# Attention weights in the memory of k, b, w and a of a recurrence, loaded and split in its last tile

## Chip, cores, metric

One core of a Trainium2 chip. The metric is the device time of one execution in microseconds (us), median over runs.

## What is computed

The reference chains three parts: a recurrence over 768 time steps with a 40x40 state for each of 4 x 8 heads, a feed-forward part with a 3-tap convolution in time and a sigmoid gate, and a causal attention with 4 experts of which the best 2 are mixed for each token.

```python
for t in range(S):                      # B=4, H=8, S=768, D=40
    y[:, :, t] = einsum('bhd,bhde->bhe', rt, state)
    Sa = einsum('bhde,bhe->bhd', state, at)
    state = state * wt[:, :, None, :] - einsum('bhd,bhe->bhde', Sa, bt) + einsum('bhd,bhe->bhde', vt, kt)
...
h = maximum(x @ w_in, 0); c = conv3(h, conv_w); x = (h * sigmoid(c)) @ w_out      # 320 -> 1024 -> 320
...
logits = x @ w_gate; topk = the 2 largest of 4; w = softmax over them
for e in range(4):                      # q, k, v of 64 columns
    a = softmax(causal(scale * (x @ wq[e]) @ (x @ wk[e]).T))
    out += (weight of e if it is in topk) * (a @ (x @ wv[e]) @ wo[e])
```

## The kernel before, in words

The recurrence is cut into NT = 12 tiles of 64 steps. For each tile n, `prep(n)` (L167) turns the loaded k, b, w and a into chunk matrices, `chain(k)` (L331) carries the state over each of its two halves (k = 2n, 2n+1), and `post(k)` (L414) forms the outputs, which go to a DRAM scratch `xs` (L462). `w` and `kb` are single tiles and `a` a pair that alternates; `F` and `g21` are scratch of `prep`. `P` is a ring of three tiles: tile n uses P[n % 3].

The feed-forward part `ff` (L517) follows a tile behind. It goes in 49 steps: of each tile of 64 tokens, four steps multiply by `w_in` (L561), filter (L594, L596), gate (L598, L599), split the result into a high and a low half (`split`, L477: ACT copies the high half, another engine subtracts it, L478 and L479) and multiply by `w_out` (L584); `halves` (L534) splits the tile's input into xh and xl at each first step. `store` (L619) writes to a DRAM scratch `x2`.

The attention has `setup_c` (L629), which allocates its pools in the memory that the recurrence gives back, and `proj` (L672), which loads tokens from `x2` as xt (L678), transposes them (L694), splits them into x, and multiplies by the weights wvg (v and gate, L703) and wqk (q and k, L712). The keys' tile `k` holds high halves and `kl` low halves, with the other expert's 64 partitions zero. `weigh` (L748), `scale`, `turn`, `values` and `result` (weights wo, L830) go over units (batch b, block i of 128 queries, pair pr of experts).

In `setup_c`, after four small constants (cidb and negm on the POOL queue, L640 and L641; cid and bef on the SP queue, L642 and L643), eight rows of weights are loaded from DRAM into three staging tiles `ws` (L647, queue SP) and split by ACT (L478) and VectorE (L479): 3 of wvg with 260 columns, 3 of wqk with 512, 2 of wo with 320. Then POOL clears the unused halves of the two `kl` tiles with four memsets (L653).

The order of work comes about in two steps. The program's order is made by generators: each `yield` gives a position in units of tiles, and `Kernel.merge` (L895) always takes the stream with the lowest position; the feed-forward part is put in by the amount of matmul work done so far. The remaining `ff` steps and `proj` are merged in `attention` (L914). Then the compiler's planner (`schedule_with_timeline_sim`, L1018) puts the instructions on each engine's queue by priority and a simulated time of its own. At run time each queue is in order: PE, DVE (VectorE), ACT (ScalarE), POOL (GpSimd), and SP, whose queue starts nearly all DMAs. Tiles are protected by semaphores; a tile in memory that a closed pool has given back waits for the work on that pool.

## Time and profile before

| | |
|---|---|
| median of 3 runs | 898.44 us (894.2 to 899.88) |
| the profiled execution | 899.17 us |
| its span, first to last instruction | 897.4 us |
| busy share of the span | PE 83%, PEld 73%, DVE 77%, ACT 64%, POOL 42% |
| chain that ended last, by engine | PE 42%, DVE 24%, ACT 11%, DMA 10%, issue 7%, POOL 4% |
| mean granted clock of TensorE | 0.923 of full speed |

Times in rows are us from the span's start unless they are marked ns. A wait is booked on the engine that stood idle, with what ended it behind the arrow. Matmul durations overlap, since matmuls are pipelined, so sums of busy PE time are an upper bound of its work.

### The profile page before, as it was taken

What the parts mean: (1) busy time and instruction counts of PE and PEld (TensorE: products, weight loads), DVE (VectorE), ACT (ScalarE), POOL (GpSimd) and SP (SyncE); (2) the same over time, 40 slices, a digit from 0 to 9 for tenths busy, and PEclk for the clock granted to TensorE, in tenths of its full rate; (3) what the DMA queues carried; (4) which work ended last, traced back from release to release, by engine and by line L of the source; (5) the groups of instructions that cost most, each with busy time, mean ns of one, the idle gap of its engine ahead of it and who ended that gap; (6) DMA issues with size and microseconds to landing.
All of it is one profiled execution on the core that took longest, in us unless ns stands there. A gap on an engine that the chain in (4) does not pass through costs nothing.

```text
span 897.4 us, 31509 instructions
## 1 busy us (share of the span) xinstructions
PE 748.3 (83%) x13112; PEld 657.7 (73%) x13112; DVE 693.9 (77%) x1541; ACT 574.4 (64%) x1355; POOL 377.6 (42%) x419
## 2 busy tenths in 40 slices
PE   1257768997988989888798879869999999999988
PEld 1146556785877977777687868859878888888876
DVE  5888896999898898787887984575677767876664
ACT  0156655866675767584758567758877666775565
POOL 6063545433335243322334242754644343443352
PEclk9999577997989799897979889979999999999999
DMA  5435673555564464545545534440011101110001
GB/s 129 94 122 125 166 167 86 134 127 127 116 158 104 99 152 108 132 99 130 129 113 120 117 86 93 90 127 16 15 46 37 46 16 31 37 38 16 23 8 38
DMA packets 143489, 81.17 MB, mean 90 GB/s; under 512 B 113859, under 2 KB 127043, under 8 KB 142387
## 3 DMA queue, kind: packets, MB, share of 16 engines
q1 hardware_dynamic: 138450, 74.34, 34.1%
q0 software_dynamic: 4896, 4.83, 2.5%
q8 instruction: 103, 1.69, 0.8%
q14 instruction: 40, 0.32, 0.1%
HBM read 51.63 MB, written 11.80 MB: 71 GB/s over the span
## 4 chain that ended last, share of the span: by engine, by line
PE 42%; DVE 24%; ACT 11%; DMA 10%; issue 7%; POOL 4%; SPq 1%; ACTq 0%; DVEq 0%; POOLq 0%
PE ps L161 8%; PE ps L561 5%; PE ps L584 5%; PE ps L815 4%; DVE cv L596 4%; PE ps L712 4%; PE ps L798 4%; PE ps L165 3%; PE ps L703 2%; PE ps L762 2%; PE ps L830 2%; DMA kb<-in_kb_e_dram 2%; DVE kb L205 2%; PE ps L763 2%; DVE Q L198 2%
## 5 line engine op out<-in xcount | busy, mean ns | idle before, releaser
L784 POOL TENSOR_TENSOR A<-A,rs 128x128 f32<-128x128 f32 (+5 forms) x96 | 87.7, 935 | 113.7 <-DVE rs L782 95.6
L596 DVE SCALAR_TENSOR_TENSOR cv<-h,cw,cv 128x256 f32<-128x256 f32 (+1 forms) x192 | 97.1, 550 | 38.5 <-ACT cv L594 37.7
L599 POOL TENSOR_TENSOR cv<-cv,h 128x512 f32<-128x512 f32 (+1 forms) x48 | 61.4, 1280 | 133.2 <-ACT cv L598 123.6
L561 PE MATMUL ps<-xl,win 128*128 128x256 f32 x384 | 97.1, 304 | 4.5 <-POOL xl L539 3.6
L561 PE MATMUL ps<-xh,win 128*128 128x256 f32 x384 | 96.5, 309 | 4.9 <-ACT xh L537 4.3
L584 PE MATMUL ps<-wout,gh 128*128 128x320 f32 x384 | 90.4, 330 | 2.6 <-ACT gh L478 2.5
L479 POOL TENSOR_TENSOR gl<-cv,gh 128x512 fp32r<-128x512 f32 x48 | 62.5, 1303 | 53.5 <-ACT gh L478 46.9
L769 ACT ACTIVATE A<-ps,nm 128x128 f32<-128x128 f32 (+5 forms) x96 | 60.7, 633 | 37.0 <-DVE nm L767 28.9
L561 PEld LDWEIGHTS ps<-xh,win 128*128 128x128 f32 x384 | 73.2, 210 | 7.0 <-ACT xh L537 4.6
L561 PEld LDWEIGHTS ps<-xl,win 128*128 128x128 f32 x384 | 73.1, 208 | 6.0 <-POOL xl L539 4.1
L767 DVE TENSOR_REDUCE nm<-ps 128x1 f32<-128x128 f32 (+5 forms) x96 | 58.8, 619 | 20.5 <-PE ps L765 8.9
L584 PEld LDWEIGHTS ps<-wout,gh 128*128 128x128 f32 x384 | 66.0, 200 | 4.9 <-ACT gh L478 4.1
L161 PE MATMUL ps<-kb,a 40*32 40x64 f32 x1536 | 34.3, 239 | 34.7 <-DVE kb L205 31.1
L584 PE MATMUL ps<-wout,gl 128*128 128x320 f32 x192 | 59.0, 330 | 0.3 <-issue 0.3
L165 PE MATMUL ps<-cst,kb 104*128 104x104 f32 x192 | 33.3, 307 | 29.4 <-ACT KB L265 16.4
L161 PE MATMUL ps<-RB,LB 104*40 104x32 f32 (+1 forms) x1536 | 47.9, 215 | 11.1 <-DMA RB<-in_rb_dram 5.0
L161 PEld LDWEIGHTS ps<-kb,a 40*32 40x32 f32 x1536 | 28.1, 120 | 39.0 <-issue 19.1
L161 PEld LDWEIGHTS ps<-RB,LB 104*40 104x40 f32 (+1 forms) x1536 | 41.6, 131 | 17.3 <-DVE cv L596 4.6
L798 PE MATMUL ps<-cid,A 128*128 128x128 f32 x336 | 52.9, 276 | 1.5 <-ACT AT L803 0.7
L762 PE MATMUL ps<-k,q 128*128 128x256 f32 (+3 forms) x144 | 49.3, 351 | 5.3 <-ACT A L769 3.8
L712 PE MATMUL ps<-x,wqk 128*128 128x384 f32 x256 | 53.2, 347 | 0.3 <-ACT yt L622 0.3
L598 ACT ACTIVATE cv<-cv 128x512 f32<-128x512 f32 (+1 forms) x48 | 30.3, 630 | 30.7 <-DVE cv L596 30.4
(177 smaller groups left out, 2191.6 us busy)
## 6 DMA issues: line engine op xcount, KB each, us to landing
kb<-in_kb_e_dram SPq DMA_DIRECT2D x24, 320.0 KB
LB<-KB SPq DMA_DIRECT2D x48, 160.0 KB
LB<-S SPq DMA_DIRECT2D x46, 100.0 KB
a<-in_a_e_dram SPq DMA_DIRECT2D x24, 160.0 KB
VT<-in_vt_dram SPq DMA_DIRECT2D x48, 80.0 KB
RB<-in_rb_dram SPq DMA_DIRECT2D x48, 80.0 KB
SV<-in_v_dram SPq DMA_DIRECT2D x48, 80.0 KB
VZ<-in_v_dram SPq DMA_DIRECT2D x96, 40.0 KB
```

What stands on the lines that cost most here:

```text
L161: self.nc.tensor.matmul(*a, **k)
L165: self.nc.tensor.transpose(*a)
L479: (eng or self.nc.vector).tensor_tensor(lo, x, hi.bitcast(F32), op=ALU.subtract)
L561: nc.tensor.matmul(hp[:, dd], wt[:, 128 * d:128 * d + 128], x, start=k == 0, stop=k == 7)
L584: nc.tensor.matmul(self.ps[1][:, tb, :DM], x, wt, start=d == 0 and k == 0, stop=d == 7 and k == 2)
L596: nc.vector.scalar_tensor_tensor(y, h[:, dd, :, k:k + nt], self.cw[:, k, d:d + 1], y, op0=ALU.mult, op1=ALU.add)
L599: (nc.gpsimd if GM and st % GM == 0 and st >= GN else nc.vector).tensor_tensor(cv[:, :, :, :nt], cv[:, :, :, :nt], h[:, :, :, 1:1 + nt], o ...
L712: nc.tensor.matmul(pp, self.wqk[:, wk, hl, 128 * m:128 * m + 128], x[:, xk], start=j == 0, stop=j == 7)
L762: nc.tensor.matmul(sp[:, c0:c1], q[:, ce, 128 * j:128 * j + 128], k[:, ce, c0:c1], start=True, stop=False)
L769: nc.scalar.activation(A[:, :nk], sp[:, :nk], AF.Exp, bias=nm, accum_out=sums[:, e:e + 1])
L784: nc.gpsimd.tensor_tensor(A[:, :nk], A[:, :nk], rs[:, e:e + 1].to_broadcast([128, nk]), op=ALU.mult)
L798: nc.tensor.transpose(tp[:, m, e], As[e][:, 128 * (2 * g + m):128 * (2 * g + m) + 128], self.cid)
```

## The change

Two tiles s0 and s1 are made in a pool `shr` of their own, which lives to the end. In the recurrence s0 holds kb and w, s1 holds a[0], F and g21 (the pair's other tile a[1] stays). A new stream `more` calls `weights_c` from position 11.0 on, in steps of 0.15 tiles up to 12.05. It takes the two tiles again as wqk (s0) and wvg and wo (s1), and stages the eight rows in the two halves of P[0] (last used by tile 9). The split's subtraction is given to POOL in place of VectorE, and wqk comes first. `setup_c` keeps the four constants and the tiles kl, without loads and memsets. The memsets of kl for batch 0 go to VectorE in `proj(0, 0)`; those for batch 1 stay on POOL, in `weigh(1, 0, 0)`, queued behind the last subtraction of `halves` (`self.cut`). `bef` is allocated earlier.

```diff
-        self.w = cp.tile([128, 32, 32], F32, name="w")
-        self.kb = cp.tile([128, 16, 2, 2, 32], F32, name="kb")
-        self.a = [cp.tile([128, 2, 2, 16, 32], F32, name=f"a{j}") for j in range(2)]
+        s0, s1 = [self.sp.tile([128, n], F32, tag=f"s{j}", name=f"s{j}", bufs=1) for j, n in enumerate((3072, 2840))]
+        self.kb = s0[:, :2048].rearrange(...)
+        self.w = s0[:, 2048:].rearrange(...)
+        self.F = s1[:, 2048:2560].rearrange(...)
+        self.g21 = s1[:, 2560:2816].rearrange(...)
+        self.a = [s1[:, :2048].rearrange(...), cp.tile([128, 2, 2, 16, 32], F32, name="a1")]
...
-        F = wk.tile([128, 16, 32], F32, name="F", bufs=1)
+        F = self.F
...
-            nc.gpsimd.tensor_tensor(xl[64:, 2], xd[64:, 2], xh[64:, 2].bitcast(F32), op=ALU.subtract)
+            self.cut = nc.gpsimd.tensor_tensor(xl[64:, 2], xd[64:, 2], xh[64:, 2].bitcast(F32), op=ALU.subtract)
...
+    def weights_c(self):
+        s0, s1 = [self.sp.tile([128, n], F32R, tag=f"s{j}", name=f"r{j}", bufs=1) for j, n in enumerate((3072, 2840))]
+        self.wqk = s0.rearrange("p (k h n) -> p k h n", k=3, h=2)
+        self.wvg = s1[:, :1560].rearrange("p (k h n) -> p k h n", k=3, h=2)
+        self.wo = s1[:, 1560:].rearrange("p (k h n) -> p k h n", k=2, h=2)
+        P = self.P[(NT - 3) % 3].rearrange("p u t -> p (u t)")
+        j = 0
+        for dst, nm, n, rows in ((self.wqk, "w_qk", 512, 3), (self.wvg, "w_vg", 260, 3), (self.wo, "w_o", DM, 2)):
+            for k in range(rows):
+                s = P[:, 512 * (j % 2):512 * (j % 2) + n]
+                j += 1
+                nc.sync.dma_start(s, self.i[nm][k])
+                self.split(dst[:, k, 0], dst[:, k, 1], s, nc.gpsimd)
+                yield
...
-        for dst, nm, n, rows in ((self.wvg, "w_vg", 260, 3), (self.wqk, "w_qk", 512, 3), (self.wo, "w_o", DM, 2)):
-            for k in range(rows):
-                s = cw.tile([128, S], F32, tag="A", name="ws", bufs=3)[:, :n]
-                nc.sync.dma_start(s, i[nm][k])
-                self.split(dst[:, k, 0], dst[:, k, 1], s)
...
-        for t in self.kl:
-            for e in range(2):
-                nc.gpsimd.memset(t[Z[1 - e], e::2].bitcast(F32), 0.0)
...
             t["kl"] = self.kl[b % 2]
+            if b == 0:
+                for e in range(2):
+                    nc.vector.memset(t["kl"][Z[1 - e], e::2].bitcast(F32), 0.0)
...
+        if (b, i, pr) == (1, 0, 0):
+            with self.tc.issue_after(self.cut.ins):
+                for e in range(2):
+                    nc.gpsimd.memset(t["kl"][Z[1 - e], e::2].bitcast(F32), 0.0)
...
+            self.sp = top.enter_context(tc.tile_pool(name="shr", bufs=1))
             self.setup_b(bctx)
...
+                def more():
+                    yield NT - 1.0
+                    for j, _ in enumerate(self.weights_c()):
+                        yield NT - 1.0 + 0.15 * (j + 1)
+
-                self.merge([links(), preps(), second(), posts(), weights()], ff)
+                self.merge([links(), preps(), second(), posts(), weights(), more()], ff)
```

## Rows read from the trace of the kernel before

**Rows 1.** Stretches: length, busy us (count) of PE, PEld, DVE, ACT, POOL; clock; DMA.

```profile
541.00:576.00 35.00, 34.31 (x776) 31.38 (x764) 19.62 (x37) 26.52 (x60) 15.18 (x15) 1.00 0.42 92
576.00:607.00 31.00, 21.23 (x128) 19.15 (x128) 20.33 (x37) 18.11 (x46) 20.54 (x20) 0.83 0.47 120
607.00:630.00 23.00, 22.36 (x159) 21.63 (x159) 11.60 (x32) 18.80 (x41) 10.95 (x13) 1.00 0.06 15
```

**Rows 2.** PE's waits from 576 to 610: total us, times, longest.

```profile
PE ps L694 <- DMA x<-yt: 5.4, 1, 5.4
PE ps L703 <- DVE lg L706: 2.5, 1, 2.5
PE ps L584 <- ACT gh L478: 0.8, 1, 0.8
```

**Rows 3.** View of stretches of 5 us, columns as in rows 1.

```profile
585.00:590.00 5.00, 2.78 (x10) 2.06 (x11) 4.32 (x5) 1.19 (x4) 2.93 (x3) 0.51 0.63 182
590.00:595.00 5.00, 4.06 (x21) 3.46 (x21) 3.77 (x8) 4.07 (x11) 1.36 (x1) 0.80 0.47 140
...
600.00:605.00 5.00, 3.13 (x15) 3.05 (x15) 1.93 (x10) 3.85 (x12) 2.64 (x3) 0.72 0.22 78
```

**Rows 4.** Timeline of SP's queue, 575 to 583: start, us, issue of the DMAs.

```profile
575.45 1.67 SPq L462 DMA_DIRECT2D xs<-xe  x2
...
580.81 1.28 SPq L647 DMA_DIRECT2D ws<-in_w_vg_dram  x3
582.13 0.43 SPq L678 DMA_DIRECT2D xt<-x  x1
```

**Rows 5.** Groups of instructions, 576 to 610: busy us, mean ns | idle before, releaser.

```profile
L653 POOL MEMSET kl<- 64x1536 f32 x4 | 5.5, 1375 | 0.2
...
L479 DVE TENSOR_TENSOR wvg<-ws,wvg 128x260 fp32r<-128x260 f32 x3 | 4.9, 1681 | 5.3 <-ACT wvg L478 5.3
...
L479 DVE TENSOR_TENSOR wqk<-ws,wqk 128x512 fp32r<-128x512 f32 x3 | 2.1, 693 | 1.9 <-ACT wqk L478 1.9
...
L478 ACT ACTIVATE wqk<-ws 128x512 fp32r<-128x512 f32 x3 | 1.9, 630 | 2.6 <-DMA ws<-in_w_qk_dram 2.6
...
L478 ACT ACTIVATE wvg<-ws 128x260 fp32r<-128x260 f32 x3 | 1.1, 408 | 2.0 <-DMA ws<-in_w_vg_dram 2.0
...
L479 DVE TENSOR_TENSOR wo<-ws,wo 128x320 fp32r<-128x320 f32 x2 | 1.0, 478 | 0.0
L478 ACT ACTIVATE wo<-ws 128x320 fp32r<-128x320 f32 x2 | 0.9, 463 | 0.0
```

**Rows 6.** Timeline of POOL, 583 to 629.

```profile
583.41 1.17 POOL L479 TENSOR_TENSOR gl<-cv,gh 128x512 fp32r<-128x512 f32 x1
...
585.69 1.44 POOL L538 TENSOR_TENSOR xl<-xd,xh 128x512 fp32r<-128x512 f32 x1
587.21 0.80 POOL L539 TENSOR_TENSOR xl<-xd,xh 64x256 fp32r<-64x256 f32 x1
...
628.23 0.76 POOL L784 TENSOR_TENSOR A<-A,rs 128x128 f32<-128x128 f32 x2 [3.62 <-DVE rs L782]
```

**Rows 7.** Timeline of PE, the matmuls around the pause.

```profile
580.10 0.75 PE L584 MATMUL ps<-wout,gh 128*128 128x320 f32 x4
586.27 0.88 PE L694 MATMUL ps<-cid,xt 128*128 128x128 f32 x3 [5.42 <-DMA x<-yt]
```

**Rows 8.** Views of tiles g and wx: ns min/median/max, first and last start.

```profile
L161 PE MATMUL ps<-O,g x768: 209/228/258, 49.5 to 540.4; 32*32 32x32 f32 x192
...
L479 POOL TENSOR_TENSOR win<-wx,win x12: 719/728/1010, 52.5 to 97.0; 128x256 fp32r<-128x256 f32 x12
```

**Rows 9.** Timeline of the last tile: loads of VZ on SP, their user on PE.

```profile
556.22 3.26 SPq L141 DMA_DIRECT2D VZ<-in_v_dram  x4
...
564.39 1.31 PE L161 MATMUL ps<-VZ,KB 128*40 128x80 f32 x32
```

**Rows 10.** View of line L81, VectorE's only large memset of SBUF.

```profile
L81 DVE MEMSET w<- x1: 912/912/912, 1.0 to 1.0; 32x1024 f32 x1
```

More of the change, by code (lines that the diff above doesn't have):

```diff
@@ L61, in setup_a @@
         self.wk = ctx.enter_context(tc.tile_pool(name="awk", bufs=2))
-        self.w = cp.tile([128, 32, 32], F32, name="w")
-        self.kb = cp.tile([128, 16, 2, 2, 32], F32, name="kb")
-        self.a = [cp.tile([128, 2, 2, 16, 32], F32, name=f"a{j}") for j in range(2)]
+        s0, s1 = [self.sp.tile([128, n], F32, tag=f"s{j}", name=f"s{j}", bufs=1) for j, n in enumerate((3072, 2840))]
+        self.kb = s0[:, :2048].rearrange("p (u b x t) -> p u b x t", u=16, b=2, x=2)
+        self.w = s0[:, 2048:].rearrange("p (u t) -> p u t", u=32)
+        self.F = s1[:, 2048:2560].rearrange("p (u t) -> p u t", u=16)
+        self.g21 = s1[:, 2560:2816].rearrange("p (u r s) -> p u r s", u=8, r=2)
+        self.a = [s1[:, :2048].rearrange("p (b h u t) -> p b h u t", b=2, h=2, u=16),
+                  cp.tile([128, 2, 2, 16, 32], F32, name="a1")]
         self.SV = cp.tile([128, 2, 2, NP, 40], F32, name="SV")
@@ L77, in setup_a @@
         self.S = [cp.tile([128, NP, 2, 40], F32, name=f"S{j}") for j in range(2)]
-        self.g21 = cp.tile([128, 8, 2, 16], F32, name="g21")
         self.d1 = cp.tile([128, 8, 32], F32, name="d1")
@@ L626, in store @@
             nc.sync.dma_start(self.x2[b, tk:tk + TOK - j0], y[64 * (b % 2) + j0:64 * (b % 2) + 64, b // 2])
+    def weights_c(self):
+        nc = self.nc
+        s0, s1 = [self.sp.tile([128, n], F32R, tag=f"s{j}", name=f"r{j}", bufs=1) for j, n in enumerate((3072, 2840))]
[11 more added lines that the diff above has]
+                yield
     def setup_c(self, ctx):
@@ L632, in setup_c @@
         cw = self.cwk = ctx.enter_context(tc.tile_pool(name="cwk", bufs=2))
-        self.wqk = cp.tile([128, 3, 2, 512], F32R, name="wqk")
-        self.wvg = cp.tile([128, 3, 2, 260], F32R, name="wvg")
-        self.wo = cp.tile([128, 2, 2, DM], F32R, name="wo")
         self.cid = cp.tile([128, 128], F32, name="cid")
+        self.bef = cp.tile([128, 4, 4], F32, name="bef")
         self.cidb = cp.tile([128, 128], BF16, name="cidb")
         self.negm = cp.tile([128, 128], BF16, name="negm")
-        self.bef = cp.tile([128, 4, 4], F32, name="bef")
         nc.gpsimd.dma_start(self.cidb, i["consts"][:, :128])
```

## Prediction, made before the run

> **What bounds the kernel now.** I read the view of stretches first, with the cuts laid where the recurrence ends and the attention begins [rows 1]. The reader is to see three regimes. In the last tile of the recurrence, 541 to 576, PE is busy 34.31 of 35 us at full clock: PE is the bound. From 607 it is so again, 22.36 of 23 us. Between lies a pause: from 576 to 607 PE is busy 21.23 of 31.0 us, so 9.77 us idle, at a mean granted clock of 0.83. What a change is worth in that stage is read from who ends PE's idle time there.
>
> The second view is PE's waits in the pause [rows 2]. Three rows make up 8.7 of the 9.77 us. The largest, 5.4 us, is the transposes of proj(0, 0), and the releaser named is a store of x2; but the transposes read xt, whose load was issued on SP at 582.13, last in a row behind three loads of wvg's staging tiles that were issued from 580.81 [rows 4]. PE starts at 586.27, 4.1 us after the issue [rows 7]. I take that for xt's landing. The second, 2.5 us, is the gate's logits on VectorE; the third, 0.8 us, is gh on ACT.
>
> The third view is the groups of the pause [rows 5]. There stands what the change takes away: ACT waits 2.0 and 2.6 us for staged weights to land and splits them in 1.1 + 1.9 + 0.9 = 3.9 us; VectorE subtracts for 4.9 + 2.1 + 1.0 = 8.0 us; POOL clears kl for 5.5 us. Behind POOL's memsets stand, from 583.41 on, gl, and then xl of the next tile of the feed-forward part until 588.0 [rows 6]. PE's last matmul before its wait ends at 580.85 [rows 7].
>
> The clock is the fourth: three stretches in the pause run below the upper level, with 2.78 us of PE at 0.51, 4.06 at 0.80 and 3.13 at 0.72 [rows 3]; 0.51 is nearly the lower level (1.2 GHz) throughout, right after the wait of 5.4 us. At full clock this work would take 1.36 + 0.81 + 0.88 = 3.05 us less. So the pause can give back at most 9.77 + 3.05 = 12.8 us.
>
> **The change, part by part.**
>
> *Weights out of the pause.* (a) The xt load follows bef on SP, without three loads ahead. It still waits for the stores of xe into xs that were issued at 575.45: the loads at 580.81 waited as well, and they go into the same given-back memory. So its issue moves from 582.13 to 580.8, its landing from 586.27 to 584.9: 1.3 us. (b) POOL has no memsets, so gl can go at about 577.8 and xl as soon as ACT has made xh at about 580.9: done at 580.9 + 1.44 + 0.80 = 583.1 in place of 588.0 [rows 6]. Then PE has sixteen matmuls of the next step and eight of the last one to put into the wait for xt. Of 5.4 us I leave 2.0, so 3.4 saved. Bounds: 1.3 (only xt comes sooner) and 5.4 (all hidden). (c) The wait of 0.8 us for gh goes, since ACT no longer stands behind wqk's landings. (d) The logits' wait of 2.5 us comes from VectorE's and ACT's queues being full; with 8.0 and 3.9 us of work less I take half, 1.2; bounds 0 and 2.5. (e) Of the clock's 3.05 us I take three quarters, 2.3, since the long wait ahead of the lowest stretch shrinks; bounds 0 and 3.05. Sum saved: 3.4 + 0.8 + 1.2 + 2.3 = 7.7 us.
>
> *Weights into the last tile.* SP: eight issues, at 1.28 / 3 = 0.43 us each 3.4 us [rows 4]. Queued behind them are the loads of the recurrence's last half tile. The nearest is VZ, issued 556.22 to 559.48, whose user on PE starts at 564.39 [rows 9], 4.9 us after the last issue; 4.1 us is what the larger xt needed to land. That leaves 0.8 us, and three or four weight loads (1.3 to 1.7 us) come ahead of it: up to 0.9 us late. A load also waits until the split before the last has left its half of P[0], and everything behind it on SP waits too. ACT: 3.9 us more in a stage with 35 - 26.52 = 8.5 free. POOL: three subtractions of 512 columns at 1.17 (gl's row), three of 260 at 0.73 (win's, 256), two of 320 at about 0.91 (win's, scaled): 7.5 us, in a stage with 35 - 15.18 = 19.8 free [rows 1, 6, 8]. PE, with no more work, stays the bound, and its full queue is the cover. Bounds: nothing, as long as PE has matmuls ready, and about 11 us (the last rival), if ACT's queue stands at loads that have not landed. I take 1.0, near the SP term. The DMAs land in tiles whose last reader ends early: g21 is read until 540.4 [rows 8], and P[0] belongs to tile 9.
>
> *Memsets of kl.* Those of batch 0 go to VectorE: 1536 columns at the rate of 1024 in 0.912 us [rows 10] are 1.37 us each, 2.7 in all; VectorE waits 5.3 us before wvg's first subtraction [rows 5], and the first use of kl is far behind. Cost 0; bound 2.7 if they stand ahead of a filter step. Those of batch 1 are 2 x 1.375 us on POOL, behind the last xl subtraction; POOL has a wait of 3.62 us before 628.23 [rows 6], which covers them. Cost 0; bound 2.75.
>
> *Shared tiles.* The recurrence's instructions stay the same; kb beside w, and F and g21 beside a[0], have separate columns. I count 0. If the planner saw conflicts between neighbours in a tile, every tile would pay, but PE reads parts of x in the pause while others are still written, so it tells columns of a tile apart.
>
> Net: 7.7 - 1.0 = 6.7 us. The profiled execution took 899.17 us around a span of 897.4; 899.17 - 6.7 = 892.5. The median of the runs shown is 0.73 lower, so on that scale 891.7 us.
>
> **A rule that speaks against it.** wvg's subtractions on VectorE took 1681 ns for 260 columns, wqk's 693 ns for 512 [rows 5]; the former ran from 583.40, while POOL did gl, cv and xl [rows 6]. The Trainium skill, SBUF — State Buffer, section Who interferes with whom, says that a VectorE instruction with two SBUF inputs and a GpSimd instruction that reads SBUF exclude each other. The trace agrees with 1681 against 693. By that rule the 7.5 us of subtractions on POOL would block filter steps and state updates in the last tile.
>
> **Rivals.**
>
> 1. *The pause closes nearly whole.* All 12.8 us come back less the 1.0: 899.17 - 11.8 = 887.4, on the scale of the runs 886.6. For it: PE has 97% of the stretch from 607 with the same mix of ff and proj, so nothing but the weights need hold it. Against: xt still lands at 584.9.
> 2. *xt and the order keep the pause.* The planner puts L694 ahead of the feed-forward matmuls, as before, and PE waits for xt, then for the logits: saved are 1.3 and 0.8, less 1.0: 898.1, on the scale 897.3. For it: SP and ACT are in order, and before too the sixteen L561 of that step stood behind proj.
> 3. *POOL and VectorE exclude each other in the last tile.* A subtraction of 260 columns was stretched from about 0.35 (half of 693) to 1.68, by 1.33 us; eight such meetings are 10.6 us of VectorE, where 15.4 are free [rows 1]. If a third stands on the chain that PE waits for, 3.5 us replace the 1.0: 899.17 - 7.7 + 3.5 = 895.0, on the scale 894.2.
> 4. *Slower: ACT's queue stands at the staged weights.* If the planner puts the splits ahead of the recurrence's copies and the loads land late, as the first load of wvg did (2.0 us of ACT's wait), eight times 2.0 are 16 us of standing. ACT has 8.5 us free less 3.9 of work, so 4.6; 11.4 us would move into the recurrence: 899.17 - 7.7 + 11.4 = 902.9, on the scale 902.2. It decides from (4.6 + 7.7) / 8 = 1.5 us of wait for each load. Against: before, ACT had nothing else to do in those waits, and the loads here are issued a tile's third ahead of one another's splits.
>
> **How the numbers follow.** Forecast (saved between 3 and 9 us) 0.44; rival 1 0.26; rival 2 0.12; rival 3 0.08; rival 4 0.10. One per cent, 9 us, is about what a measurement of this kernel tells from no change. Faster by more than that (below 889.5) are rival 1 and the lower end of the forecast, 0.26 + 0.08 = 0.34. Slower by more (above 907.4) is rival 4 with the memsets' 2.75 us and more loads in the way: 0.05. The rest, 0.61, is within. The range goes from 884 (the ceiling, 898.44 - 12.8 = 885.6, and a little for a changed order in what follows) to 902, rival 4's own time; some 0.15 is left out.
>
> **What would show it.** In the profile after: no L647; ACT's and POOL's splits into wqk, wvg and wo between 536 and 570, with short waits for DMA; POOL's gl and xl before 584; xt issued within 0.5 us of 580.8 less any shift; PE's idle in the pause about 4 us in place of 9.77, with no stretch at 0.5; the end of the recurrence (xs from xe, 575.45) no more than 1 us later. The prediction is wrong if that end moves by over 3 us, if ACT waits over 1.5 us for each staged row, or if PE's wait for xt stays above 4 us.

## Result, and the profile after

The change makes the kernel slower: 901.46 us (median of 20 runs, 894.71 to 905.99) against 895.32 us for the kernel before, measured beside it (20 runs, 887.5 to 903.24). The ratio is 1.0072, with a 95% interval of 1.0052 to 1.0091, so some 6.4 us are lost where 6.7 were forecast as a gain. The profiled execution took 903.48 us around a span of 901.7 (before: 899.17 and 897.4). Line numbers in the changed kernel are mostly three higher; its weights are the tile `r`, loaded on L645 and split on L481 (ACT) and L482 (POOL). The profiled executions of e3 and e11 below were slow ones, so no stage times are taken from them.

Up to the last two tiles of the recurrence the compiled order of every engine is that of before, so any difference there (1.5 us in favour of the change) is that of two executions. The time is cut from there on in four stages: the last two tiles (from the transposes T of tile 10 on VectorE to the last issue of xs from xe), the pause (to the first matmul by wqk), the rest of the feed-forward part (to the issue of x from z), and the attention alone. "Mixed" below is the pause and the rest together. Stretches of the kernel before, columns as in [rows 1]:

```profile
498.20:575.45 77.25, 69.16 (x1513) 62.77 (x1513) 55.25 (x97) 52.43 (x115) 28.59 (x29) 0.91 0.41 91
575.45:607.30 31.85, 22.08 (x135) 20.00 (x134) 20.83 (x39) 18.75 (x47) 21.09 (x20) 0.84 0.46 117
607.30:655.80 48.50, 45.53 (x323) 41.68 (x322) 29.25 (x73) 38.99 (x89) 26.54 (x30) 1.00 0.06 14
655.80:897.40 241.60, 229.42 (x1937) 195.85 (x1935) 167.56 (x498) 157.32 (x436) 100.30 (x120) 1.00 0.10 31
```

The same four stages of the changed kernel:

```profile
496.67:583.17 86.50, 74.59 (x1519) 67.21 (x1519) 56.21 (x97) 56.04 (x123) 36.38 (x37) 0.86 0.43 97
583.17:605.21 22.04, 17.83 (x121) 16.62 (x120) 13.70 (x29) 13.20 (x35) 14.25 (x14) 0.92 0.40 100
605.21:662.80 57.59, 51.27 (x348) 47.33 (x346) 34.15 (x92) 49.01 (x106) 30.65 (x35) 0.94 0.05 12
662.80:901.70 238.90, 227.63 (x1921) 194.15 (x1920) 164.59 (x484) 154.40 (x427) 100.00 (x120) 1.00 0.10 32
```

Read down the lengths: +9.25, -9.81, +9.09, -2.70. The pause gives back what was hoped for and more; the last two tiles take as much, and the rest of the feed-forward part takes it once more. Where the pause ends is a mark in a new order, so its split from the rest is soft: over the mixed stage as a whole idle time falls from 12.74 to 10.53 us, with some 4 us for the clock in both.

**The last tile.** The stretch of [rows 1], and four short ones in it, of the changed kernel:

```profile
541.00:576.00 35.00, 30.63 (x599) 27.29 (x600) 13.04 (x25) 23.19 (x51) 15.13 (x15) 0.85 0.45 106
...
551.00:556.00 5.00, 2.38 (x42) 2.10 (x38) 2.05 (x3) 3.34 (x7) 2.59 (x3) 1.00 0.65 177
556.00:561.00 5.00, 3.79 (x33) 2.99 (x32) 0.00 (x0) 3.52 (x8) 2.64 (x3) 0.54 0.58 133
561.00:566.00 5.00, 5.00 (x28) 4.54 (x28) 3.69 (x6) 2.36 (x6) 0.87 (x1) 0.50 0.55 110
566.00:571.00 5.00, 5.00 (x203) 4.48 (x203) 0.69 (x1) 2.87 (x7) 2.37 (x2) 0.93 0.27 60
```

From 541 to 576 PE is idle for 35.00 - 30.63 = 4.4 us, against 0.7 before, and runs at 0.85 instead of 1.00, which costs 30.63 x 0.15 = 4.6 us: 3.7 + 4.6 = 8.3 us, in this execution the whole delay of the recurrence's end (from T of tile 11 it took 40.9 us instead of 32.7). The clock stands at its lower level (1.2 GHz) right behind a stretch in which PE was busy only 2.38 of 5 us. What made that hole is seen in the timelines of SP, ACT and PE, in this order:

```profile
548.45 2.01 SPq L645 DMA_DIRECT2D P<-in_w_vg_dram  x2
...
548.21 1.42 ACT L379 ACTIVATE VZ<-ps 32x640 f32<-32x640 f32 x2
551.87 0.89 ACT L481 ACTIVATE r<-P 128x260 fp32r<-128x260 f32 x2 [2.23 <-DMA P<-in_w_vg_dram]
552.78 1.90 ACT L397 ACTIVATE U<-VZ 32x320 f32<-32x320 f32 x4
...
554.74 0.65 PE L168 MATMUL ps<-cst,U 128*104 128x128 f32 x4 [2.62 <-ACT U L397]
```

ACT is through with VZ at 549.6 and could copy U from it. Ahead of U in its queue stand two splits whose rows have not landed: it stands for 2.23 us and works 0.89 us on them, and PE waits 2.62 us for U. The waits of ACT from 541 to 586 (total, times, longest) show all landings that it stood at in this stage, 5.4 us in four waits:

```profile
ACT r L481 <- DMA P<-in_w_vg_dram: 2.2, 1, 2.2
ACT r L481 <- DMA P<-in_w_o_dram: 1.7, 2, 1.0
ACT r L481 <- DMA P<-in_w_qk_dram: 1.5, 1, 1.5
```

PE's waits of the same stretch; before, it waited 0.7 us in all from 541 to 575, and for none of these:

```profile
PE ps L168 <- ACT U L397: 2.6, 1, 2.6
PE ps L587 <- ACT gh L481: 1.2, 1, 1.2
PE ps L164 <- ACT M L326: 0.9, 1, 0.9
PE ps L587 <- POOL gl L482: 0.5, 1, 0.5
```

**Pause and rest.** PE's waits from 583 to 605, which answer to [rows 2]:

```profile
PE ps L705 <- DMA xt<-x: 2.5, 1, 2.5
PE ps L714 <- DVE lg L717: 0.8, 1, 0.8
```

5.4 and 2.5 us have become 2.5 and 0.8. PE's idle time in the pause falls from 31.85 - 22.08 = 9.77 to 22.04 - 17.83 = 4.21 us, and the clock's share from 22.08 x 0.16 = 3.5 to 17.83 x 0.08 = 1.4. PE's waits from 605 to 663:

```profile
PE ps L587 <- ACT gh L481: 3.7, 3, 1.7
PE ps L587 <- ACT yt L625: 1.3, 1, 1.3
PE ps L723 <- DVE q L731: 1.2, 1, 1.2
```

In the rest, idle time grows from 2.97 to 6.32 us, the clock (0.94 instead of 1.00) takes 51.27 x 0.06 = 3.1 us, and 25 more matmuls are in it (of the 14 by `win` that the pause has fewer, 6 are here). The chain of the page's part 4 tells the same in one line: PE's share went from 42% to 37%, ACT's from 11% to 17%.

```profile
PE 37%; DVE 25%; ACT 17%; DMA 9%; issue 7%; POOL 3%; SPq 2%; DVEq 0%; ACTq 0%; POOLq 0%
```

One thing in ACT's groups differs that no step of the prediction had: loads of function tables, each of 1283 ns, as ACT goes from the gate's sigmoid to the softmax's exp and back. The largest groups before (9 loads in all):

```profile
L598 ACT ACT_TABLE_LOAD x4 | 5.1, 1283 | 0.1
L769 ACT ACT_TABLE_LOAD x3 | 3.8, 1283 | 0.1
```

and after (13 in all):

```profile
L601 ACT ACT_TABLE_LOAD x6 | 7.7, 1283 | 0.1
L784 ACT ACT_TABLE_LOAD x5 | 6.4, 1283 | 0.1
```

### The profile page after: what moved, and what is told of

Its sections match the earlier page's. It is cut to its first block, busy times and chain, and to the rows that moved or that the text cites. A ratio compares the mean times of both kernels' runs of the same rounds, so it can differ in the third digit from the quotient of the medians.

```text
span 901.7 us, 31514 instructions
## 1 busy us (share of the span) xinstructions
PE 753.0 (84%) x13112; PEld 663.1 (74%) x13112; DVE 690.1 (77%) x1535; ACT 579.1 (64%) x1359; POOL 375.7 (42%) x425
## 4 chain that ended last, share of the span: by engine, by line
PE 37%; DVE 25%; ACT 17%; DMA 9%; issue 7%; POOL 3%; SPq 2%; DVEq 0%; ACTq 0%; POOLq 0%
PE ps L164 6%; PE ps L830 5%; PE ps L723 4%; PE ps L587 4%; DVE cv L599 4%; PE ps L813 3%; PE ps L564 3%; PE ps L168 2%; PE ps L777 2%; PE ps L845 2%; DVE Q L201 2%; PE ps L714 2%; ACT U L397 2%; ACT A L784 2%; PE ps L778 2%
## 5 line engine op out<-in xcount | busy, mean ns | idle before, releaser
L587 PE MATMUL ps<-wout,gh 128*128 128x320 f32 x384 | 95.4, 343 | 7.5 <-ACT gh L481 5.4
L482 POOL TENSOR_TENSOR gl<-cv,gh 128x512 fp32r<-128x512 f32 x48 | 63.9, 1332 | 47.8 <-ACT gh L481 46.9
L587 PEld LDWEIGHTS ps<-wout,gh 128*128 128x128 f32 x384 | 69.6, 211 | 10.0 <-ACT gh L481 6.5
L587 PE MATMUL ps<-wout,gl 128*128 128x320 f32 x192 | 61.4, 341 | 0.5 <-POOL gl L482 0.5
L723 PE MATMUL ps<-x,r 128*128 128x384 f32 x256 | 54.3, 353 | 1.4 <-DVE q L731 1.2
L168 PE MATMUL ps<-cst,s 104*128 104x104 f32 x192 | 32.6, 302 | 25.1 <-ACT KB L268 14.1
L379 ACT ACTIVATE VZ<-ps 32x640 f32<-32x640 f32 x48 | 33.5, 697 | 23.8 <-PE ps L164 22.8
L830 PE MATMUL ps<-AT,v 128*64 128x128 f32 x672 | 47.3, 280 | 1.5 <-ACT AT L818 1.5
```

The lines of the kernel that those rows point to most:

```text
L482: (eng or self.nc.vector).tensor_tensor(lo, x, hi.bitcast(F32), op=ALU.subtract)
L587: nc.tensor.matmul(self.ps[1][:, tb, :DM], x, wt, start=d == 0 and k == 0, stop=d == 7 and k == 2)
L723: nc.tensor.matmul(pp, self.wqk[:, wk, hl, 128 * m:128 * m + 128], x[:, xk], start=j == 0, stop=j == 7)
L830: nc.tensor.matmul(op[64 * e:64 * e + 64], v[:, kt, 128 * pr + 64 * e:128 * pr + 64 * e + 64], ATs[kt][:, e], start=kt == n - 1, stop=kt = ...
```

## Experiments

Theory 1: the last tile is lost because the splits stand in ACT's queue ahead of what PE waits for. For the rest of the feed-forward part, theory A blames POOL's memset of the second kl, theory B the four more table loads. Stages are in us, of each kernel's profiled execution; "behind" is from the recurrence's end to the end of the span. The change, e1, e7, e13 and e15 have the same order on VectorE, ACT and POOL in the last two tiles, and still take 81.8 to 87.1 us there: a difference of a few us between two single executions decides nothing by itself.

| | ratio to before, 95% interval | last two tiles | mixed | behind | table loads |
|---|---|---|---|---|---|
| before | | 77.2 | 80.3 | 321.9 | 9 |
| the change | 1.0072 (1.0052 to 1.0091) | 86.5 | 79.6 | 318.5 | 13 |
| e1 memsets back | 1.0218 (1.0179 to 1.0257) | 81.8 | 92.3 | 333.4 | 15 |
| e2 memsets alone | 1.0023 (0.9986 to 1.0060) | 78.0 | 82.0 | 322.1 | 9 |
| e3 weights late | 1.0077 (1.0036 to 1.0117) | | | | 13 |
| e4 loads ahead | 1.0016 (0.9986 to 1.0047) | 83.3 | 79.0 | 316.0 | 11 |
| e5 weights behind | 1.0128 (1.0095 to 1.0162) | 79.3 | 74.0 | 327.5 | 7 |
| e6 one table, before | 0.9990 (0.9953 to 1.0027) | 76.6 | 75.6 | 317.6 | 2 |
| e7 one table, change | 1.0029 (0.9996 to 1.0063) | 84.7 | 74.7 | 314.2 | 2 |
| e8 ahead, VectorE | 1.0015 (0.9986 to 1.0044) | 80.5 | 80.5 | 319.7 | 13 |
| e9 two loads | 1.0021 (0.9992 to 1.0050) | 82.1 | 80.5 | 317.8 | 11 |
| e10 VectorE copies | 1.0086 (1.0054 to 1.0118) | 84.3 | 78.2 | 317.5 | 13 |
| e11 tanh, before | 0.9951 (0.9920 to 0.9981) | | | | 3 |
| e12 ahead, VectorE, tanh | 0.9961 (0.9938 to 0.9984) | 79.1 | 74.8 | 312.3 | 3 |
| e13 no memset on POOL | 1.0072 (1.0038 to 1.0106) | 84.2 | 79.7 | 318.6 | 13 |
| e14 ahead, POOL, tanh | 1.0030 (0.9986 to 1.0075) | 78.6 | 75.5 | 317.3 | 3 |
| e15 tanh, change | 1.0001 (0.9960 to 1.0043) | 87.1 | 76.3 | 313.9 | 3 |

**e1, the memsets put back.**

```diff
+        for t in self.kl:                       # setup_c, as before
+            for e in range(2):
+                nc.gpsimd.memset(t[Z[1 - e], e::2].bitcast(F32), 0.0)
...
-                    nc.vector.memset(...)       # proj(0, 0)
-                    nc.gpsimd.memset(...)       # weigh(1, 0, 0)
```

> The change, with the four memsets of kl put back on POOL where they were. Three markers cut the time: the last tile (VectorE's transposes T to the last issue of xs from xe; 32.7 us before, 40.9 after), the pause (from there to the first matmul by wqk; 31.9 before, 22.0 after) and the rest (from there to the end of the span; 290.1 before, 296.5 after). Theory A for the 6.4 us lost in the rest: POOL's memset of 2.8 us ahead of cv and gl at 622.7, and the clock's fall behind it; then the rest returns to 290 to 292 here and the pause grows by 1 to 3. Theory B: the planner's new order mixes sigmoid and exp on ACT more finely, with 13 loads of function tables of 1.28 us against 9; this kernel alternates no less often, so the rest stays at 295 to 299. The last tile stays near 41 under both. Ratio to the kernel before: A 1.001 to 1.004, B 1.006 to 1.012.

Measured: 1.0218, far outside both. Behind the recurrence 333.4 us, 14.9 more than in the change. POOL's memsets again stand ahead of gl and xl in the pause, and in the mixed stage PE waits for xt, the softmax's A and gh. Taking the weights out of the pause and leaving the memsets in it is worse than leaving both. Theory A, as put, falls; B's bracket was too low, though 15 table loads are the most of all.

**e2, the memsets alone**, moved as in the change, in the kernel before.

```diff
-        for t in self.kl: ... nc.gpsimd.memset(...)      # setup_c
+                    nc.vector.memset(...)                # proj(0, 0)
+                    nc.gpsimd.memset(...)                # weigh(1, 0, 0), behind self.cut
```

> The kernel before with the move of kl's memsets alone. The compiled order of ACT alternates between sigmoid and exp as often as before. Theory A (the memset on POOL costs the rest of the run): the rest grows from 290.1 to 294 to 297, ratio 1.003 to 1.007. Theory B (table loads): the rest stays within 1 us of 290.1 with 9 table loads, and POOL, free in the pause, gives back 0 to 3 us there: ratio 0.996 to 1.000. The last tile is that of before, 32.7, under both.

Measured: 1.0023, an interval that holds no change; behind the recurrence 322.1 against 321.9 us. A's 4 to 7 us are not there in this execution; the interval alone would leave room for 5.

**e3, weights late in the program.**

```diff
-                self.merge([links(), preps(), second(), posts(), weights(), more()], ff)
+                self.merge([links(), preps(), second(), posts(), weights()], ff)
+                for _ in self.weights_c():
+                    pass
```

> The change with the shared tiles, the staging in P, POOL's subtractions and the moved memsets, but with the loads and splits issued behind the recurrence's last tile. Theory 1 (the last tile is lost because ACT's queue stands at staged rows that have not landed, and the clock falls after PE's waits): the last tile returns to 32.5 to 33.5, the pause to 28 to 33. Rival (the shared tiles s0 and s1 themselves, or kb beside w, cost the recurrence): the last tile stays at 36 to 41 and all tiles ahead of it are longer too. The compiled order alternates between sigmoid and exp as often as the change does: theory B then wants 295 to 298 in the rest, theory A 295 to 297 as well (POOL's memset is where the change put it). Ratio under theory 1 about 1.005.

The edit did not do what it says: the planner, which orders by priority and readiness, pulled the loads up again. SP's queue in this kernel's trace, in the last tile:

```profile
544.64 0.36 SPq L645 DMA_DIRECT2D P<-in_w_vg_dram  x1
```

So it tells nothing of theory 1, and its ratio, 1.0077, is that of the change. A position in the generators is no fence; only a dependence holds work back, which e5 uses.

**e4, all rows staged ahead**, no half of P[0] used twice.

```diff
+        Q = self.wk.tile([128, 32, 32], F32, tag="Q", ...)     # two halves; P[0] two; two tiles wy
+        for s, (nm, n, k) in zip(slots, rows):
+            nc.sync.dma_start(s, self.i[nm][k])
+            yield
...
+            self.split(dst[nm][:, k, 0], dst[nm][:, k, 1], s, nc.gpsimd)
...
-                    yield NT - 1.0
+                    yield NT - 1.48                            # loads by 0.06, splits from NT - 1.0
```

> The change with all eight rows staged in memory of their own (two halves of Q, two of P, and two tiles wy), loaded from position 10.52 on, and split by ACT and POOL from 11.0 on as in the change. Theory 1 (ACT stands at landings): ACT's waits for staged rows go from 5.5 us in all to under 1, PE waits under 1 us for U, M and gh together, no stretch at a clock of 0.5, last tile 33 to 35. Rival (ACT's own work of 3.9 us of splits ahead of U, M and gh delays PE): the waits for landing go but the last tile keeps 37 to 41. Rival (SP's queue: the loads of the last half tile come late): PE waits for VZ or KB, last tile 36 to 40. Pause 20 to 24. Alternation of sigmoid and exp: 11 table loads, so by theory B a rest of 292 to 295. Ratio under theory 1 with B 0.993 to 0.999.

ACT stands at no landing any more, and the ratio falls to 1.0016, below the change's interval, but the last two tiles keep 83.25 us. ACT now does its eight copies almost in one block, from 540.4 to 545.9, and PE waits for VT, KB, U and gh 5.9 us in the two tiles. Of these, 3.2 us are for VT and KB, for which PE waits 3.3 us before too; the 2.7 us for U and gh are new. The first rival is the nearer one. The clock is low here from 538 to 548 us (0.72 and 0.60), but the copies are not shown to be the reason: PE's wait for VT ends before the first of them, and e6, which splits nothing there, has that wait and a low stretch behind it too. The stage's line, the wait and the first copies, then e6:

```profile
498.08:581.33 83.25, 71.55 (x1535) 64.73 (x1530) 58.63 (x97) 54.91 (x121) 36.40 (x36) 0.88 0.43 96
...
538.41 0.33 PE L164 MATMUL ps<-ra,VT 104*64 104x64 f32 x2 [1.69 <-ACT VT L433]
...
540.39 1.15 ACT L481 ACTIVATE r<-Qz 128x512 fp32r<-128x512 f32 x2
```

```profile
534.44 0.33 PE L161 MATMUL ps<-ra,VT 104*64 104x64 f32 x2 [1.73 <-ACT VT L430]
...
536.00:541.00 5.00, 4.87 (x216) 4.34 (x215) 2.18 (x6) 3.68 (x10) 0.97 (x1) 0.66 0.08 21
```

**e5, weights behind the recurrence by a dependence.**

```diff
-        P = self.P[(NT - 3) % 3].rearrange("p u t -> p (u t)")
+        P = self.P[(NT - 1) % 3].rearrange("p u t -> p (u t)")     # with the edit of e3
```

> The change with the staging moved from P[0], free since tile 9, to P[2], which the recurrence's last multiplication still reads: by that alone no load of the weights can start before the recurrence ends. Shared tiles, POOL's subtractions and the moved memsets stay. The time is cut in four stages by the transposes T of tile 10 on VectorE, the last issue of xs from xe, and the last issue of x from z (the end of the feed-forward part): the last two tiles of the recurrence took 77.2 us before and 86.5 in the change, the mixed stage behind them 80.3 and 79.6, the attention alone 241.7 and 238.9. Theory 1 (it is the weights in the last tile that cost the recurrence): the last two tiles return to 76.5 to 79. Rival (the shared tiles or something else of the change costs it): 82 to 87. Theory B (the mixed stage pays for the loads of function tables): this order alternates 6 times, with 7 or fewer table loads against 9 before and 13 in the change, so the mixed stage, though it has the weights' pause again, takes 76 to 81. Against B: 82 to 86. Ratio to the kernel before by theory 1 with B: 0.992 to 1.000.

Its last two tiles:

```profile
497.73:577.03 79.30, 71.12 (x1506) 63.80 (x1505) 57.25 (x97) 52.23 (x113) 30.50 (x30) 0.89 0.44 95
```

79.3 us, just above theory 1's bracket and far below the rival's: it is the weights that cost the recurrence, the shared tiles do not. The ratio is 1.0128, because the staging through two halves now stands in the pause in full (behind the recurrence 327.5 us). From the other side that gives an idea of what the change's pause is worth: 327.5 - 318.5 = 9.0 us, though the orders differ behind it. The mixed stage of 74.0 us is no evidence for B: it ends sooner since it holds 401 matmuls, not 466, and the attention makes up for it.

**e6 and e7, one function table** in both kernels, all orders kept.

```diff
-        nc.scalar.activation(ex, ex, AF.Exp)
+        nc.scalar.activation(ex, ex, AF.Sigmoid)
...
-            nc.scalar.activation(A[:, :nk], sp[:, :nk], AF.Exp, bias=nm, accum_out=...)
+            nc.scalar.activation(A[:, :nk], sp[:, :nk], AF.Sigmoid, bias=nm, accum_out=...)
```

> The kernel before with the attention's exp (in the mixing weights and in the softmax) replaced by sigmoid: this changes what is computed, the softmax's numerators. All engines' orders stay as they are, but ACT keeps one function table: 7 of 9 table loads are gone, 9.0 us of ACT. If table loads cost their time only on ACT, off the path: ratio 0.998 to 1.001. If ACT is the bound of the mixed stage, where it is busy 57 of 80 us before, they cost 3 to 9 us: ratio 0.990 to 0.997, mixed stage 72 to 78 in place of 80.3.

> The same edit in the changed kernel: exp replaced by sigmoid in the attention, all orders as in the change, 11 of 13 table loads gone, 14.1 us of ACT. Theory B (the change loses in the mixed stage what its pause gives, because of 4 more table loads): the mixed stage shrinks by 5 us more than it does in the kernel before under the same edit, to 66 to 72, and this kernel stands 0 to 4 us above that one in all, what the last tile costs less what the pause gives. Rival (the clock's fall and the new order of the work cost the mixed stage, whatever the tables): the mixed stage shrinks no more than in the kernel before, and this kernel stands 5 to 8 us above that one, as the change does. Ratio to the kernel before: theory B 0.985 to 0.993, rival 0.996 to 1.004.

The mixed stages of the two, first the kernel before, then the change:

```profile
572.97:648.60 75.63, 64.86 (x449) 59.83 (x448) 51.91 (x111) 48.31 (x129) 47.93 (x50) 0.93 0.24 58
```

```profile
575.00:649.70 74.70, 67.00 (x464) 62.65 (x463) 50.80 (x119) 47.48 (x129) 45.62 (x50) 0.95 0.15 39
```

The time behind the recurrence falls by 321.9 - 317.6 = 4.3 us without 7 loads and by 318.5 - 314.2 = 4.3 us without 11. So in these executions table loads cost both kernels, and over these stages the change no more than the other: the 3.4 us between the two stay 3.4. By that, theory B falls as the reason of the lost gain. The ratios (0.999, the value for loads off the path, and 1.0029, the rival's) are nearer to each other than 1.0072, but their intervals are too wide to tell 5 us from none.

**e8, ahead and copied by VectorE.**

```diff
-            self.split(dst[nm][:, k, 0], dst[nm][:, k, 1], s, nc.gpsimd)
+            nc.vector.tensor_copy(dst[nm][:, k, 0], s)
+            nc.gpsimd.tensor_tensor(dst[nm][:, k, 1], s, dst[nm][:, k, 0].bitcast(F32), op=ALU.subtract)
```

> The kernel with the rows staged ahead in memory of their own, and the high halves copied by VectorE in place of ACT; POOL still subtracts. With the rows ahead but the copies on ACT the last two tiles took 83.2 us against 77.2 before, and PE's waits for ACT (VT, KB, U, gh) 5.9 us. Theory 1, sharpened: what is in the way is ACT's queue, by its copies as much as by its standing at landings; then PE's waits for ACT in these two tiles fall to under 4 us and they take 76.5 to 79.5. Rival (SP's eight loads and POOL's subtractions are in the way): 81 to 85, with PE waiting for RB, VZ or gl. The alternation of sigmoid and exp is that of the change, so the mixed stage takes 78 to 81. Ratio under theory 1: 0.994 to 1.000, under the rival 0.999 to 1.005.

Its last two tiles:

```profile
495.96:576.43 80.47, 71.17 (x1514) 64.09 (x1515) 59.43 (x105) 52.33 (x115) 37.27 (x36) 0.89 0.44 96
```

PE's waits for ACT here are 4.1 us (KB 1.8, VT 1.3, gh 0.5, hc 0.3, yt 0.2), about what theory 1 wanted and 0.5 more than before (KB 3.1, hc 0.3, VT 0.2), with none for U. The last two tiles take 80.5 us, 1 above its bracket. The mixed stage takes 80.5 us, so the whole stands at 1.0015: in the rival's bracket for the ratio, and no better than e4.

**e9, two of eight rows loaded.**

```diff
-                nc.sync.dma_start(s, self.i[nm][k])
+                if j < 3:
+                    nc.sync.dma_start(s, self.i[nm][k])
```

> The change with only the first two of the eight rows loaded, one into each half of P[0]; the other six loads are left out, so the eight splits on ACT and POOL all work on those two rows and six rows of weights have wrong values. All of ACT's 3.9 us and POOL's 7.5 us of splitting stay in the last tile; what goes are six landings to stand at and six issues on SP. If landings and SP's issues are what costs the recurrence: last two tiles 77 to 80 us (77.2 before, 86.5 and 84.7 in the change's order). If ACT's and POOL's work itself is what costs it, as the 83.2 us with all rows staged ahead suggest: 81 to 85, with PE's waits for ACT (VT, KB, U, X, gh) 5 to 8 us in these tiles. The mixed stage alternates 10 times: 77 to 81. Ratio to the kernel before: 0.994 to 1.000 by the first, 0.998 to 1.004 by the second.

82.1 us and 1.0021: with no landings to stand at and two issues on SP, ACT's and POOL's work alone keeps some 3 to 5 us in this execution. PE's waits for ACT are 5.2 us (KB 1.8, gh 1.5, VT 1.3, U 0.6), of which the 2.1 for gh and U are new. It agrees with e4 by another way.

**e10, VectorE's copies with the loads in place.**

```diff
-                self.split(dst[:, k, 0], dst[:, k, 1], s, nc.gpsimd)
+                nc.vector.tensor_copy(dst[:, k, 0], s)
+                nc.gpsimd.tensor_tensor(dst[:, k, 1], s, dst[:, k, 0].bitcast(F32), op=ALU.subtract)
```

> The change with one edit: VectorE copies the high halves in place of ACT, the loads stay as they are, one behind the other's split in two halves of P[0]. If what costs the recurrence is that ACT, in order, has the splits ahead of the copies that PE waits for, be it by standing or by working: PE's waits for ACT in the last two tiles fall under 5 us, and they take 78 to 82, as with the rows staged ahead and VectorE's copies (80.5). If VectorE's queue now stands at the landings in ACT's place and filter steps and state updates wait behind it: 83 to 88, with PE waiting for sT, RB or s on VectorE. The mixed stage has the change's alternation (12): 79 to 81. Ratio 0.998 to 1.004 by the first, 1.004 to 1.010 by the second.

VectorE's waits in its last two tiles, then PE's longest:

```profile
DVE r L646 <- DMA P<-in_w_vg_dram: 7.8, 2, 5.4
DVE r L646 <- DMA P<-in_w_o_dram: 4.9, 2, 4.5
```

```profile
PE ps L587 <- ACT gh L481: 3.7, 1, 3.7
```

VectorE stands for 12.7 us at landings in ACT's place; behind it wait the filter steps, behind these the sigmoid and gh, and PE stands for 3.7 us at gh. 84.3 us and 1.0086: the second case. Moving the copies alone moves the standing.

**e11, e12 and e15, tanh gates.** The same gate, with tanh in the last steps, in the kernel before, in e8's and in the change.

```diff
-                nc.scalar.activation(cv[...], cv[...], AF.Sigmoid)
+                if st < 40:                       # 39 in e12 and e15
+                    nc.scalar.activation(cv[...], cv[...], AF.Sigmoid)
+                else:
+                    nc.scalar.activation(cv[...], cv[...], AF.Tanh, scale=0.5)
+                    nc.vector.tensor_scalar(cv[...], cv[...], 0.5, 0.5, op0=ALU.mult, op1=ALU.add)
```

> The kernel before with the gates of the steps from 40 on worked out as 0.5 tanh(c/2) + 0.5, the multiplication and addition on VectorE: the same function, and the Trainium skill, ScalarE: Activation LUTs, section Table sets: the hidden batching unit, has tanh in one set with exp. So ACT alternates between two sets once, with 2 table loads against 9. With exp replaced by sigmoid in the kernel before, 7 fewer table loads gave 4.7 us of the mixed stage at an order that stayed the same. Here VectorE has some 9 steps more of 128 x 512, and the planner lays a new order. If table loads are what limits the mixed stage: 74 to 78 us in place of 80.3, ratio 0.993 to 0.998. If the new order decides: 78 to 86, ratio 0.998 to 1.006.

> The kernel with the rows staged ahead and copied by VectorE (last two tiles 80.5 us), with the gates of the steps from 39 on by tanh as in the other kernel: 2 table loads against 13. With exp replaced by sigmoid, the change's mixed stage fell from 79.6 to 74.7 us. If the parts add up: last two tiles 79 to 82, from the recurrence's end to the end of the span 312 to 317 (321.9 before, 318.5 in the change), ratio 0.990 to 0.997, faster than both kernels. If VectorE's additional work in the last tiles or the new order takes it back: last two tiles 82 to 87 or 317 to 323 behind them, ratio 0.998 to 1.006.

> The change with the gates of the steps from 39 on by tanh: 2 or 3 table loads against 13, everything else as the change has it. The kernel before gained 0.49% by the same means (ratio 0.9951). If the change's two losses are independent, the last two tiles keep 82 to 86 and the stages behind them fall from 318.5 to 311 to 315: ratio 0.999 to 1.004. If the table loads were part of the last tile's loss as well, or if the mixed stage of the change gains more than that of the kernel before: below 0.998.

ACT's groups in e12 have three table loads in all: the first of the kernel, one for sigmoid, and one at the mixing weights' exp, after which tanh and exp share a set. The last two:

```profile
L602 ACT ACT_TABLE_LOAD x1 | 1.3, 1283 | 0.0
L748 ACT ACT_TABLE_LOAD x1 | 1.3, 1283 | 0.0
```

e11 gains 0.49%. The change gains about the same by it, from 1.0072 to 1.0001, and keeps its last two tiles (87.1 us, 1 above the bracket), as it should if the two losses are independent. e12 is faster than both kernels (0.9961), and the parts add up as expected; its last two tiles and mixed stage:

```profile
497.44:576.56 79.12, 71.50 (x1514) 64.28 (x1515) 59.86 (x105) 52.36 (x115) 37.31 (x37) 0.89 0.44 98
576.56:651.40 74.84, 67.54 (x491) 63.48 (x490) 55.29 (x135) 50.66 (x136) 47.00 (x51) 1.00 0.16 39
```

But e11, without any of the change, is as fast: the gain is that of the tables, and the change, even with its last tile mended, is worth nothing measurable beside it.

**e13, no memset on POOL.**

```diff
-            with self.tc.issue_after(self.cut.ins):
-                for e in range(2):
-                    nc.gpsimd.memset(t["kl"][Z[1 - e], e::2].bitcast(F32), 0.0)
+            for e in range(2):
+                nc.vector.memset(t["kl"][Z[1 - e], e::2].bitcast(F32), 0.0)
```

> The change with the memsets of the second kl tile on VectorE in place of POOL, without the order behind the last subtraction: the planner puts them among VectorE's first work behind the recurrence. In the change's trace they stand on POOL from 622.67 to 625.48, directly ahead of a gate product and its low half, and the granted clock falls right there. The last two tiles keep the change's order. If those memsets are what gives the pause's gain back: the stage from the first matmul by wqk to the feed-forward part's end falls from 57.6 to 52 to 55 us, the mixed stage to 74 to 77. If it is the order in which feed-forward steps, projections and softmax meet (12 alternations of tables stay): 57 to 60 and 78 to 82. Ratio to the kernel before: 1.001 to 1.005 by the first, 1.006 to 1.010 by the second.

Ratio 1.0072, mixed stage 79.7 us, the time of the change in both: the memset is not the cause, though it stood where the clock fell. (The stage from the first matmul by wqk on falls to 53.0 us, into the bracket that blamed the memsets; but that matmul comes 4.7 us later after the recurrence here, so the mixed stage as a whole is what compares.)

**e14, both halves split by POOL**, ahead and with tanh.

```diff
-            nc.vector.tensor_copy(dst[nm][:, k, 0], s)
+            nc.gpsimd.tensor_copy(dst[nm][:, k, 0], s)
```

> The rows staged ahead in memory of their own, both halves of the split by POOL (copy and subtraction), and the gates of the steps from 40 on by tanh. With VectorE's copies the last two tiles took 80.5 and 79.1 us, against 76.1 to 79.3 in five kernels that split no weights there. If VectorE's copies are the remainder: 76 to 78.5 here. If SP's loads and POOL's work are: 79 to 82, with PE waiting for gl, which POOL makes. Mixed stage with 2 alternations 74 to 80. Ratio 0.988 to 0.995 by the first, 0.994 to 1.000 by the second.

Its last two tiles:

```profile
492.22:570.80 78.58, 72.22 (x1563) 65.42 (x1564) 59.01 (x101) 54.20 (x119) 44.67 (x46) 0.91 0.46 101
```

POOL is busy 44.67 us in place of 28.59, and the last two tiles take 78.6 us, within the 76.6 to 79.3 of the kernels without weights there (before, e2, e5, e6), if above the bracket by a hair. As a whole it is unclear (1.0030), with an interval wider than the effect; behind the recurrence it takes 317.3 us against 312.3 in e12, so POOL is not shown to be the better place.

## Why the prediction was wrong

**Right: the pause.** Forecast were 5.4 us less of PE's idle time and 2.3 us of the clock, 7.7 in all. Measured: 9.77 - 4.21 = 5.6 and 3.5 - 1.4 = 2.1, 7.7 in all. That the sum is met to a tenth is in part luck: by the single waits, xt gave 2.9 of the 3.4 us, the logits 1.7 of the 1.2, and the two errors cancel. xt is issued 588.34 - 583.17 = 5.2 us after xs, against 6.7 before [rows 4], as step (a) said:

```profile
588.34 0.39 SPq L686 DMA_DIRECT2D xt<-x  x1
```

**Wrong: "I take 1.0, near the SP term" for the last tile.** It cost some 7 us: the last two tiles take 81.8 to 87.1 us in the five kernels with the splits on ACT and the loads in place (the change, e1, e7, e13, e15), against 76.6 to 79.3 without (before, e2, e5, e6). In each of the five PE waits for U, 1.2 to 2.6 us; in none of the four does it. The 1.0 was taken for loads of the recurrence that come late, and in the profiled execution PE's waits of the tile hold no load at all. The step that failed is the cover: "PE, with no more work, stays the bound, and its full queue is the cover". PE had matmuls left, but those next in its order needed U, and U stood behind the splits. 8.5 us of free time on ACT, the number that the bound and rival 4 went by, say how much work fits in a stage, not where in the chain it is put.

What of the splits costs: standing at landings does; with VectorE copying in both, all runs of e10 and e8 say so (1.0086 and 1.0015), and e4 and e9 (1.0016 and 1.0021 against 1.0072) agree, though their order behind the recurrence differs a little too. (The last two tiles of e4 and e9 alone do not tell it: 83.2 and 82.1 us lie inside the spread of the five.) That the copies themselves cost on ACT is read from single executions and not shown: those of e4 and e9, with new waits for U and gh, against 80.5, 79.1 and 78.6 us in e8, e12 and e14, while the runs of e8 are no faster than those of e4.

In the profiled execution the clock then doubled the price, 3.7 us of idle time to 8.3; no step had it. How much it takes differs between executions: in e1, with the same order there, PE waited 2.33 us for U and had the full clock back by 560.

```profile
555.70 0.66 PE L168 MATMUL ps<-cst,U 128*104 128x128 f32 x2 [2.33 <-ACT U L397]
...
555.00:560.00 5.00, 4.10 (x32) 3.61 (x34) 0.00 (x0) 3.44 (x9) 2.80 (x3) 0.66 0.76 175
560.00:565.00 5.00, 5.00 (x110) 4.35 (x105) 3.05 (x6) 3.84 (x9) 1.77 (x2) 1.00 0.46 96
```

**Rival 4 came near in its number by luck, and in its reason by half.** Its 902.2 was 3.8 us above a before of 898.44; beside the 901.46 the kernel before took 895.32, and the loss was 6.4. It put the whole loss into the recurrence; measured, a part of it is in the rest of the feed-forward part. The queue that stands is ACT's, as it said. Its condition was wrong: it decides from 1.5 us of wait per load, and ACT waited 5.4 us for eight rows, 0.7 each. One wait of 2.23 us in the wrong place was enough. The loads follow one another's splits more closely than thought: each half of P[0] serves four times, so a load waits for POOL's subtraction two rows back, and ACT for the load.

**Rival 3 is hardly seen.** POOL's subtractions took 3.8 + 2.8 + 1.7 = 8.3 us against the 7.5 estimated. VectorE is busy 56.21 us with its 97 instructions of the last two tiles, 0.96 more than before, where the rival had up to 10.6, and PE's wait for POOL in the tile is 0.5 us:

```profile
L482 POOL TENSOR_TENSOR r<-P,r 128x512 fp32r<-128x512 f32 x3 | 3.8, 1284 | 10.4 <-ACT r L481 10.4
L482 POOL TENSOR_TENSOR r<-P,r 128x260 fp32r<-128x260 f32 x3 | 2.8, 930 | 4.5 <-DMA P<-in_w_vg_dram 4.5
L482 POOL TENSOR_TENSOR r<-P,r 128x320 fp32r<-128x320 f32 x2 | 1.7, 864 | 4.6 <-ACT r L481 4.6
```

And with 16 us more of POOL in e14 the tiles take 78.6 us. By the rule of the Trainium skill, SBUF — State Buffer, section Who interferes with whom, POOL's reads in those 16 us contend with VectorE's instructions of two SBUF inputs; the filter steps on VectorE took 624 ns each in e14 and in the change, against 586 before, so the trace agrees in kind. What of it reached PE does not stand out from the spread of single executions here.

**Rivals 1 and 2** are excluded by the pause itself: 4.2 us of idle time are left in it (rival 1 wanted about none), and xt's wait is halved (rival 2 wanted 4.1 us left).

**Wrong: nothing behind the pause.** Idle time and clock in the rest of the feed-forward part take 3.35 + 3.1 = 6.4 us of the 7.7 back. The prediction had no term for that stage. What the runs speak against: the memsets (e2, e13), and in the sum the table loads (e6, e7: 4.3 us in either kernel; without the loads the two kernels stay 0.4 to 0.5% apart, e6 and e7 as well as e11 and e15, though the intervals overlap). Of the rest alone the table loads do explain a part: without its ten loads it falls from 57.6 to 52.5 us in the change, without its six from 48.5 to 45.4 before, so four more loads are 2 of the 6.4 us; before, the one load in the pause was worth 1.6 there, which evens the sums. The other 4 are open; that the planner's new order of steps and projections makes new waits (gh, yt, q), behind which the clock falls, is read from the trace, and no run here holds the order and takes those waits away.

## What to carry to other kernels

A stage with free time on an engine is not a place to put work: look at what stands next in that engine's in-order queue and who waits for it. Work with a transfer in front gets staging in memory of its own, loaded well ahead, so that no queue stands at it: with that the loss fell from 0.72% to 0.16% (e4). Another engine for the copy without it gained nothing (e10), and on top of it nothing that the runs can tell (e8). A pause that closes is worth only what the stage behind it does not lose again, so predict up to the next point where both kernels must have done the same work.

## What was not expected of the hardware

- One wait of 2.6 us was followed by some ten microseconds at a clock of 0.54 and 0.50, with PE busy 3.79 and 5.00 of 5 us in them. In that execution the clock cost more than the wait; in e1 a wait of 2.3 us was followed by less than five microseconds below the full clock.
- A table load is 1283 ns in every row. The Trainium skill, ScalarE: Activation LUTs, section What ACT_TABLE_LOAD costs, has the same figure, and about 2.66 us for a switch with its drain. Seven loads less gave 4.3 us behind the recurrence in the kernel before, 0.6 each, and eleven less 4.3 us in the change, 0.4 each: less than half of a load's time reached the end here. The Trainium skill, ScalarE: Activation LUTs, section Table sets: the hidden batching unit, has tanh in one set with exp; e11's and e12's three loads agree.
